# Relu² attention feeding a capacity-routed FFN: paired heads on TensorE tiles, whole-batch loads, an on-chip broadcast and a hand-written issue order

## The chip, the core and the metric

The kernel runs on one core of a Trainium2 chip. The metric is device time in microseconds of one execution; lower is better. Three runs of the kernel before gave 380.47, 383.15 and 383.99 us, with a median of 383.15 us.

## What is computed

Eight batches, 12 heads of 448 tokens with head dimension 64. The attention has no softmax: the scores are clipped at zero and squared. Its output, laid out as 448 tokens of 768 features, is the input x of a mixture-of-depths layer: a gate vector scores each token, the 128 best tokens of each batch go through a two-matrix FFN, and their result, scaled by the sigmoid of the score, is added to x.

```python
scores = np.matmul(q, k.transpose(0, 1, 3, 2)) / 8
attn = np.maximum(scores, 0.0) ** 2 / 448
x = np.matmul(attn, v)                      # heads side by side: 8 x 448 x 768
s = np.einsum('bsd,d->bs', x, w_gate)
top = 128 tokens of largest s, per batch
out = x.copy()
out[top] += sigmoid(s[top]) * (np.maximum(x[top] @ w1, 0) @ w2)    # w1 768x1024, w2 1024x768
```

## The kernel before

The unit of work is a pair of heads: six pairs per batch, 48 in all. Tokens are cut into four chunks of 112 (`NCH`, `P`), four tokens of a row to a partition.

`load_qkv_pair` issues three DMAs per pair from POOL's queue, which also convert float32 to bf16: q and k as 112 partitions of eight 64-element pieces (L104 for the first two pairs, in four DMAs each; L106 else), v as 112 partitions of two 256-element pieces (L107). The FFN weights `w1_sb` and `w2_sb` (L84, L86) are loaded behind the first pair's data.

`attention_pair` transposes q and k of both heads on TensorE (L121, eight products of 112 columns against the identity) and copies the result to SBUF on VectorE (L129). Then each head in turn makes its scores, two chunks of keys to a PSUM tile `s_psum` (L140: 64 contraction rows, 112 keys, 448 queries); ScalarE clips the tile (L150; every twelfth on VectorE, L153), VectorE squares it (L156), and TensorE multiplies it into `oT_psum` (L161: 112 rows, 64 output columns, 448 queries), the first head into partitions 0 to 63, the second into 64 to 127. ScalarE copies the pair's output to `xT_sb` (L167).

`assemble_x` makes the gate scores as one row (L173), copies the row out of PSUM (L179), stores it to DRAM (L180) and transposes x back to token order (L186, copied by VectorE in L192). `moe_batch` reads the scores back from DRAM twice, as columns (L196) and broadcast to 128 partitions (L199); VectorE counts each token's rank (L206) and makes a one-hot matrix (L214), which TensorE transposes (L220, copied in L227); L231 and L235 make the sigmoid. Then TensorE gathers the 128 tokens (L244, copied by ScalarE in L249) and runs the FFN (L259, relu L264; L272, scaled copy L277). The result is scattered back by a product with the transposed one-hot (L284), added to x on VectorE (L289), and x is stored by POOL's queue (L297; the last batch in four pieces, L295).

Nothing in the text sets the order between these parts: the tile framework's scheduler orders each engine's instructions by priority and free buffers (`qk` 4, `qt` 3, `s_psum` 2, `m_psum` 2), and every DMA of POOL's queue uses one of eight semaphores in turn, so that a DMA is issued only when the eighth before it has landed.

Of the kernel before, what the change touches and what calls it, by code (L numbers as in the profile page):

```python
# [9 lines left out]
FP32 = mybir.dt.float32  # L10
# [4 lines left out]
ALU = mybir.AluOpType  # L15


@with_exitstack
def kernel(
# [11 lines left out]
    nc = tc.nc  # L31
# [6 lines left out]
    NCH = S // P  # L38
    NDC = HD // 128
    NFC = F // 128  # L40
    assert S == NCH * P

    o_scale = 1.0 / (Dh * S)

    RELU_DVE_EVERY = 12
    SQUARE_2TILE = True

    const_pool = ctx.enter_context(tc.tile_pool(name="const", bufs=1))
    qk_pool = ctx.enter_context(tc.tile_pool(name="qk", bufs=4))
    qt_pool = ctx.enter_context(tc.tile_pool(name="qt", bufs=3))  # L50
    a_pool = ctx.enter_context(tc.tile_pool(name="a", bufs=5))
    xt_pool = ctx.enter_context(tc.tile_pool(name="xt", bufs=2))
    x_pool = ctx.enter_context(tc.tile_pool(name="x", bufs=2))
    moe_pool = ctx.enter_context(tc.tile_pool(name="moe", bufs=3))
    small_pool = ctx.enter_context(tc.tile_pool(name="small", bufs=3))

    qt_psum_pool = ctx.enter_context(tc.tile_pool(name="qt_psum", bufs=1, space=bass.MemoryType.PSUM))
    s_psum_pool = ctx.enter_context(tc.tile_pool(name="s_psum", bufs=2, space=bass.MemoryType.PSUM))
    o_psum_pool = ctx.enter_context(tc.tile_pool(name="o_psum", bufs=1, space=bass.MemoryType.PSUM))
    m_psum_pool = ctx.enter_context(tc.tile_pool(name="m_psum", bufs=2, space=bass.MemoryType.PSUM))  # L60

# [12 lines left out]

    iotac_i32 = const_pool.tile([128, 1], INT32)
    nc.gpsimd.iota(iotac_i32, pattern=[[0, 1]], base=1, channel_multiplier=1)
    slot_col = const_pool.tile([128, 1], FP32)
    nc.vector.tensor_copy(out=slot_col, in_=iotac_i32)

    w1_sb = const_pool.tile([128, NDC, F], BF16)  # L80
    w2_sb = const_pool.tile([128, NFC, HD], BF16)

    def load_moe_weights():
        nc.gpsimd.dma_start(out=w1_sb,  # L84
                            in_=moe_w1.rearrange("(m p) f -> p m f", p=128))
        nc.gpsimd.dma_start(out=w2_sb,  # L86
                            in_=moe_w2.rearrange("(m p) f -> p m f", p=128))

    scores_dram = dram_pool.tile([B, S], FP32)

    out_ch = out.rearrange("b (p four) d -> b p four d", four=NCH)

    def load_qkv_pair(b, hp):
        h0 = 2 * hp
        qp = qk_pool.tile([P, NCH, 2, Dh], BF16, name="qp")
        kp = qk_pool.tile([P, NCH, 2, Dh], BF16, name="kp")
        vp = qk_pool.tile([P, 2, NCH, Dh], BF16, name="vp")
        split_load = (b == 0 and hp < 2)
        for t_sb, t_dram in ((qp, q), (kp, k)):
            src_ap = t_dram[b, h0:h0 + 2].rearrange(  # L100
                "hh (p four) d -> p four hh d", four=NCH)
            if split_load:
                for c in range(NCH):
                    nc.gpsimd.dma_start(out=t_sb[:, c], in_=src_ap[:, c])  # L104
            else:
                nc.gpsimd.dma_start(out=t_sb, in_=src_ap)  # L106
# [239 lines left out]
```

## Time and profile before

| | |
|---|---|
| median of 3 runs | 383.15 us (380.47 to 383.99) |
| the profiled execution, first to last instruction (span) | 403.7 us |
| TensorE busy (its matmuls), weight loads | 354.8 us (88%), 169.2 us |
| VectorE, ScalarE, GpSimd busy | 237.0 us (59%), 209.1 us (52%), 157.1 us (39%) |
| DMA packets, data | 108188, 32.91 MB |

The profiled execution is one run under the hardware profiler, and its span is longer than the median by 20.5 us; the trace shows nothing outside the span. Busy time is the time in which an engine had an instruction under way. Matmuls overlap and their ends are modelled, so a busy TensorE is not one at its peak. GB/s counts the bytes written, which for a load that converts are half of those read.

### The profile page before, as it was taken

The numbers are of one execution on the slowest core, as the hardware profiler recorded it, in microseconds if no ns is written. First come the engines' busy times: TensorE is split into PE (matmuls) and PEld (weight loads), VectorE is DVE, ScalarE is ACT, GpSimd is POOL, SyncE is SP. The second block draws the span as 40 slices with busy tenths as digits, with TensorE's granted clock in tenths as the row PEclk, the third lists the DMA queues.
The fourth block names the chain that finished last, engine by engine and source line by source line (L and its number), as shares of the span: only waits on it lengthen the run. The fifth ranks groups of instructions, "written<-read, shape, count | busy, mean of one in ns | idle before, by whom it ended". The sixth has DMA issues, their size and how long they took to land.

```text
span 403.7 us, 5755 instructions
## 1 busy us (share of the span) xinstructions
PE 354.8 (88%) x2192; PEld 169.2 (42%) x2192; DVE 237.0 (59%) x474; ACT 209.1 (52%) x290; POOL 157.1 (39%) x178
## 2 busy tenths in 40 slices
PE   1717999999999999998999999999999999997483
PEld 0202333343644464445434543455345534542271
DVE  0302453345466876678468846874688468946423
ACT  1403354444565846683657565846576657655121
POOL 9419655412034813571158225720573063000002
PEclk9999999999999999998999999989999999999568
DMA  5999999536029952995199809970899199103004
GB/s 26 171 168 99 75 74 65 45 38 57 2 22 194 111 41 23 194 109 42 12 195 100 62 11 198 99 61 11 185 85 87 13 185 82 21 2 136 23 2 137
DMA packets 108188, 32.91 MB, mean 82 GB/s; under 512 B 93353, under 2 KB 106161, under 8 KB 107377
## 3 DMA queue, kind: packets, MB, share of 16 engines
q0 software_dynamic: 103280, 30.68, 66.1%
q1 hardware_dynamic: 4880, 1.86, 2.3%
q8 instruction: 17, 0.28, 0.3%
q14 instruction: 11, 0.08, 0.1%
HBM read 41.17 MB, written 11.02 MB: 129 GB/s over the span
## 4 chain that ended last, share of the span: by engine, by line
PE 51%; issue 17%; DMA 13%; DVE 10%; POOL 5%; ACT 2%; POOLq 0%; SPq 0%; DVEq 0%
PE s_psum L140 14%; PE oT_psum L161 13%; DMA scores_bc<-scores_dram 6%; DMA w_sb<-in_moe_w_dram 5%; PE hT_psum L259 4%; PE ye_psum L272 4%; PE qt_psum L121 4%; PE delta_psum L284 3%; DVE a_sb L156 3%; PE xeT_psum L244 3%; DVE cmp_trash L206 3%; PE x_psum L186 2%; PE sc_psum L173 2%; DVE qkt L129 2%; DVE t_sb L153 1%
## 5 line engine op out<-in xcount | busy, mean ns | idle before, releaser
L150 ACT ACTIVATE t_sb<-s_psum 112x896 bf16<-112x896 f32 x176 | 155.1, 916 | 84.7 <-PE s_psum L140 80.0
L156 DVE TENSOR_TENSOR a_sb<-t_sb 112x896 bf16<-112x896 bf16 x192 | 113.6, 620 | 49.5 <-ACT t_sb L150 49.4
L140 PE MATMUL s_psum<-qkt 64*112 64x448 bf16 x384 | 118.6, 416 | 4.6 <-ACT t_sb L150 2.5
L161 PE MATMUL oT_psum<-a_sb,vp 112*64 112x448 bf16 x384 | 104.1, 405 | 7.3 <-ACT xT_sb L167 4.4
L107 POOL DMA_DIRECT2D vp<-in_v_dram x48 | 42.6, 888 | 118.2 <-PE oT_psum L161 110.5
L106 POOL DMA_DIRECT2D qp<-in_q_dram x46 | 62.1, 1356 | 47.5 <-PE qt_psum L121 47.2
L106 POOL DMA_DIRECT2D kp<-in_k_dram x46 | 71.7, 1580 | 10.9 <-PE qt_psum L121 9.1
L289 DVE TENSOR_TENSOR x_sb<-delta_psum,x_sb 112x384 bf16<-112x384 f32 x64 | 34.6, 556 | 47.9 <-PE delta_psum L284 46.4
L140 PEld LDWEIGHTS <-qkt 64*112 64x112 bf16 x384 | 39.0, 137 | 56.5 <-issue 46.6
L129 DVE COPY qkt<-qt_psum 128x896 bf16<-128x896 bf16 x48 | 29.8, 620 | 36.9 <-PE qt_psum L121 33.8
L161 PEld LDWEIGHTS <-vp 112*64 112x64 bf16 x384 | 29.0, 115 | 47.2 <-issue 37.7
L167 ACT ACTIVATE xT_sb<-oT_psum 128x448 bf16<-128x448 f32 x48 | 26.1, 544 | 38.7 <-PE oT_psum L161 38.1
L121 PE MATMUL qt_psum<-ident,qp 112*128 112x112 bf16 x192 | 23.4, 231 | 16.3 <-DMA qp<-in_q_dram 16.2
L121 PEld LDWEIGHTS <-qp 112*128 112x128 bf16 x192 | 13.5, 104 | 37.0 <-DMA qp<-in_q_dram 18.3
L121 PE MATMUL qt_psum<-ident,kp 112*128 112x112 bf16 x192 | 25.1, 231 | 3.4 <-DMA kp<-in_k_dram 3.2
L249 ACT CAST xeT_sb<-xeT_psum 128x384 bf16<-128x384 f32 x16 | 7.6, 477 | 36.7 <-PE xeT_psum L244 36.7
L259 PE MATMUL hT_psum<-xeT_sb,w_sb 128*128 128x128 bf16 x384 | 25.9, 227 | 0.2 <-ACT xeT_sb L249 0.2
L192 DVE COPY x_sb<-x_psum 112x768 bf16<-112x768 bf16 x32 | 17.2, 554 | 13.9 <-PE x_psum L186 13.3
L259 PEld LDWEIGHTS <-w_sb 128*128 128x128 bf16 x384 | 23.6, 103 | 3.0 <-issue 3.0
L206 DVE TENSOR_SCALAR_CACHE_REDUCE cmp_trash<-scores_bc,scores_cols 112x448 bf16<-112x448 f32 x32 | 21.6, 674 | 4.8 <-DMA scores_bc<-scores_dram 4.8
L186 PE MATMUL x_psum<-ident,xT_sb 128*112 128x128 bf16 x192 | 23.5, 250 | 0.3 <-ACT scores_row L179 0.3
L272 PE MATMUL ye_psum<-w_sb,hT_sb 128*128 128x384 bf16 x128 | 23.5, 327 | 0.3
(40 smaller groups left out, 226.9 us busy)
## 6 DMA issues: line engine op xcount, KB each, us to landing
out_dram<-x_sb POOLq DMA_DIRECT2D x7, 1344.0 KB, 6.4
vp<-in_v_dram POOLq DMA_DIRECT2D x48, 112.0 KB, 3.9
qp<-in_q_dram POOLq DMA_DIRECT2D x46, 112.0 KB, 3.7
kp<-in_k_dram POOLq DMA_DIRECT2D x46, 112.0 KB, 4.3
w_sb<-in_moe_w_dram POOLq DMA_DIRECT2D x2, 1536.0 KB, 16.1
scores_bc<-scores_dram SPq DMA_DIRECT2D x8, 224.0 KB
out_dram<-x_sb POOLq DMA_DIRECT2D x4, 336.0 KB, 2.6
qp<-in_q_dram POOLq DMA_DIRECT2D x8, 28.0 KB, 9.9
```

The source lines that it names most:

```text
L106: nc.gpsimd.dma_start(out=t_sb, in_=src_ap)
L107: nc.gpsimd.dma_start(out=vp, in_=v[b, h0:h0 + 2].rearrange("hh (p four) d -> p hh four d", four=NCH))
L121: nc.tensor.matmul(out=qt_psum[:, tno, c * P:(c + 1) * P], lhsT=t_all[:, c, :, :], rhs=ident[:P, :P], is_transpose=True, start=(i_tr == 0) ...
L129: nc.vector.tensor_copy(out=qkt, in_=qt_psum)
L140: nc.tensor.matmul(out=s_psum[:, u, :S], lhsT=kt[rows, jc * P:(jc + 1) * P], rhs=qt[rows, :], start=True, stop=True)
L150: nc.scalar.activation(out=t2_sb, in_=s_psum[:, :, :S], func=AF.Relu)
L156: nc.vector.tensor_tensor(out=a2_sb, in0=t2_sb, in1=t2_sb, op=ALU.mult)
L161: nc.tensor.matmul(out=oT_psum[rows, :], lhsT=vp[:, hh, jc, :], rhs=a2_sb[:, u, :], start=(jc == 0), stop=(jc == NCH - 1))
L206: nc.vector.tensor_scalar(out=cmp_trash, in0=scores_bcast, scalar1=scores_cols[:, c:c + 1], scalar2=None, op0=ALU.is_ge, op1=ALU.add, accu ...
L259: nc.tensor.matmul(out=hT_psum[:, fc, :], lhsT=w1_sb[:, m, fi * 128:(fi + 1) * 128], rhs=xeT_sb[:, m, :], start=(m == 0), stop=(m == NDC - 1))
L272: nc.tensor.matmul(out=ye_psum, lhsT=hT_sb[:, fi, :], rhs=w2_sb[:, fi, dd0:dd0 + ddn], start=(fi == 0), stop=(fi == NFC - 1))
L289: nc.vector.tensor_tensor(out=x_sb[:, c, dd0:dd0 + ddn], in0=delta_psum, in1=x_sb[:, c, dd0:dd0 + ddn], op=ALU.add)
```

## The change

The kernel is written anew. In the parts that matter here:

- Chunks of keys are 128 rows. 448 keys are three and a half chunks; the half chunks of two heads share the fourth, one in partitions 0 to 63 and the other in 64 to 127, with zeros in the other half (`zero_halves`).
- Scores of two heads are issued next to each other, one on contraction rows 0 to 63 and one on 64 to 127 (L180); the shared chunk is one product over all 128 rows (L184). The products with v alternate between output partitions 0 to 63 and 64 to 127 (L204). The transposes do so too, with 64 columns of weights (L159, L165).
- q, k and v are loaded a batch at a time into three sets of buffers, in nine DMAs of 256- or 192-element pieces (`load`); the first batch in three parts. The weights stand behind batch 0 and before batch 1, and batch b+2 is loaded when batch b starts.
- The gate weights are repeated over 128 columns (`wg_rep`), so that the scores come out on all 128 partitions (L221, L224); the columns are made by four small transposes (L239). The scores' trip through DRAM goes away.
- x is stored before the FFN (L269). The FFN's result is added to the 128 rows in DRAM by a scatter-add DMA (L330), whose row numbers are a product of the one-hot with token numbers (L280 to L287). The products and additions of L284 and L289 go away, as do the one-hot's transposes.
- Every relu is on ScalarE (L192), every square on VectorE (L193).
- The order of issue is the order of the text (`manual_schedule`): per pair t the scores of chunks 0 and 1, the rest of the pair before, the transposes of pair t+1, a piece of the FFN of the batch before, the scores of chunks 2 and 3, the first half of its own v products, another piece. `moe(b)` is a generator that yields the cost of each piece, and `advance` runs pieces as credit allows.

```diff
+    NBUF = 3
+    def load_q(b, h0, h1):
+        nc.gpsimd.dma_start(out=q_sb[b % NBUF][:, h0:h1],
+            in_=q[b, h0:h1].rearrange("h (p c) d -> p h c d", c=NC))
+    def load_kv(t_sb, src, b, h0, h1):
...
+        for par in range(2):
+            hs = slice(h0 + par, h1, 2)
+            lo, hi = (4, 3) if par == 0 else (3, 4)
+            nc.gpsimd.dma_start(out=t[0:64, hs, 0:lo, :],
+                in_=src[b, hs, 0:64 * lo].rearrange("h (p c) d -> p h c d", c=lo))
+            nc.gpsimd.dma_start(out=t[64:128, hs, 0:hi, :],
+                in_=src[b, hs, 64 * lo:S].rearrange("h (p c) d -> p h c d", c=hi))
...
+    load(0, 2, 6)
+    load(0, 6, H)
...
+    nc.gpsimd.dma_start(out=w1_sb, in_=moe_w1.rearrange("(m p) f -> p m f", p=128))
+    nc.gpsimd.dma_start(out=w2_sb, in_=moe_w2.rearrange("(m p) f -> p m f", p=128))
+    load(1, 0, H)
...
+    def transposes(t):
...
+        for c in range(NC):
+            for hh in range(2):
+                nc.tensor.matmul(out=ps[64 * hh:64 * hh + 64, c * P:(c + 1) * P],
+                                 lhsT=qs[:, h0 + hh, c, :], rhs=ident[:P, :P], is_transpose=True,
...
+    def scores(t, c):
...
+        if c < 3:
+            for hh in range(2):
+                rows = slice(64 * hh, 64 * hh + 64)
+                nc.tensor.matmul(out=ps[:, hh, :S], lhsT=sb[rows, S + c * 128:S + (c + 1) * 128],
+                    rhs=sb[rows, :S], start=True, stop=True)
+        else:
+            nc.tensor.matmul(out=ps[:, 0, :S], lhsT=sb[:, S + 384:S + 512],
+                             rhs=sb[:, :S], start=True, stop=True)
+    def attend(t, c):
...
+        for hh in range(2):
+            rows = slice(64 * hh, 64 * hh + 64)
+            nc.tensor.matmul(out=o_ps[t][rows, :], lhsT=vs[:, 2 * hp + hh, c, :],
+                             rhs=a[:, hh if c < 3 else 0, :], start=(c == 0),
...
+    def moe(b):
+        for m in range(NM):
+            nc.tensor.matmul(out=sc_ps, lhsT=wg_rep[:, m, :], rhs=xTb[:, m, :],
+                             start=(m == 0), stop=(m == NM - 1))
+        nc.scalar.copy(out=bc, in_=sc_ps)
+        yield 1.1
...
+            nc.vector.scalar_tensor_tensor(
+                out=trash, in0=bc[:P, :], scalar=cols[:, c:c + 1], in1=tie[:, c, :],
+                op0=ALU.subtract, op1=ALU.is_ge, accum_out=rank[:, c:c + 1])
...
+        nc.gpsimd.dma_start(out=out[b].rearrange("(p c) d -> p c d", c=NC), in_=x_sb)
...
+        nc.gpsimd.indirect_dma_start(out=out.rearrange("b s d -> (b s) d"),
+            out_offset=bass.IndirectOffsetOnAxis(ap=idx[:, :1], axis=0),
+            in_=gye, in_offset=None, element_offset=b * S * HD, compute_op=ALU.add)
...
+    MOE_US = 9.7
+        share = MOE_US / (2 * NHP) * 1.05
+        for t in range(NT + 1):
+            b, hp = divmod(t, NHP)
+            if t < NT:
+                scores(t, 0)
+                scores(t, 1)
+                relu_square(t, 0)
+                relu_square(t, 1)
+            if t > 0:
+                attend(t - 1, 2)
+                attend(t - 1, 3)
+                if t % NHP == 0:
+                    active.append(moe(t // NHP - 1))
+            if t < NT:
+                if hp == 0 and b + 2 < B:
+                    load(b + 2, 0, H)
+                if t + 1 < NT:
+                    transposes(t + 1)
+                advance(share)
+                scores(t, 2)
+                scores(t, 3)
...
+                attend(t, 0)
+                attend(t, 1)
+                advance(share)
```

TensorE in the kernel before, the first pair: `s_psum_146` takes two chunks of the first head's scores (from the transposed q and k in `qkt`), `s_psum_155` two of the second head's, and then the first head's products with v begin.

```order
L140 LDWEIGHTS qkt_134
L140 MATMUL s_psum_146<-qkt_134 112x448
L140 LDWEIGHTS qkt_134
L140 MATMUL s_psum_146<-qkt_134 112x448
L140 LDWEIGHTS qkt_134
L140 MATMUL s_psum_155<-qkt_134 112x448 [waits Activation_49]
L140 LDWEIGHTS qkt_134
L140 MATMUL s_psum_155<-qkt_134 112x448
L161 LDWEIGHTS vp_115 [waits DMASW1_49]
L161 MATMUL oT_psum_136<-a2_sb_140,vp_115 64x448 [waits DVE_49]
```

TensorE now, the second pair of batch 1 (t = 7): the scores of chunk 2 for both heads, those of the shared chunk 3, and the v products of chunks 0 and 1.

```order
L180 LDWEIGHTS qkt_585
L180 MATMUL s_ps_705<-qkt_585 128x448 [waits Activation_49]
L180 LDWEIGHTS qkt_585
L180 MATMUL s_ps_705<-qkt_585 128x448
L184 LDWEIGHTS qkt_585
L184 MATMUL s_ps_708<-qkt_585 128x448 [waits Activation_49]
L204 LDWEIGHTS v_sb1_96
L204 MATMUL o_ps_718<-a_sb_643,v_sb1_96 64x448 [waits Activation_49]
L204 LDWEIGHTS v_sb1_96
L204 MATMUL o_ps_718<-a_sb_643,v_sb1_96 64x448
```

Neighbouring products now belong to different heads, and each group of them is of another tile shape than the group before it: half the rows, all rows, half the columns.

POOL's queue in the kernel before, at the start: the weights, the second pair (in pieces) and the third, each DMA behind a semaphore of an earlier one.

```order
L84 DMA w1_sb_108<-in_moe_w1_dram 128x6x1024 [waits DMASW2_49]
L86 DMA w2_sb_109<-in_moe_w2_dram 128x8x768 [waits DMASW3_49]
L104 DMA qp_176<-in_q_dram 112x2x64 [waits DMASW4_49]
...
L104 DMA kp_177<-in_k_dram 112x2x64 [waits DMASW3_49]
L107 DMA vp_178<-in_v_dram 112x2x256 [waits DMASW4_49]
L106 DMA qp_237<-in_q_dram 112x8x64 [waits DMASW5_49]
```

POOL's queue now: the weights, batch 1, (batch 2 follows), the loads of batch 3, and behind them the first small casts of batch 0's routing (`tok0`, from the score columns `cols`) and its store.

```order
L117 DMA w1_sb_146<-in_moe_w1_dram 128x6x1024 [waits DMASW4_49]
L118 DMA w2_sb_147<-in_moe_w2_dram 128x8x768 [waits DMASW5_49]
L80 DMA q_sb1_94<-in_q_dram 112x12x256 [waits DMASW6_49]
L89 DMA k_sb1_95<-in_k_dram 64x6x256 [waits DMASW7_49]
...
L80 DMA q_sb0_91<-in_q_dram 112x12x256 [waits DMASW0_49,PE_49]
L89 DMA k_sb0_92<-in_k_dram 64x6x256 [waits DMASW1_49,PE_49]
...
L92 DMA v_sb0_93<-in_v_dram 64x6x256 [waits DMASW0_49,PE_49]
L245 CAST tok0_174<-cols_628 112x4 [waits DVE_49]
...
L269 DMA out_0_dram<-x_sb_587 112x3072 [waits DMASW1_49,DVE_49]
```

Where a pair's three DMAs stood, a batch's nine stand, and the routing's casts stand behind the last of the nine, which waits for the first of them to land.

## Rows read from the trace of the kernel before

**Rows 1.** Busy time of each engine in one batch period of the middle (windows).
```profile
core 0: us, PE busy (x) PEld busy (x) DVE busy (x) ACT busy (x) POOL busy (x), PEclk, DMA share, GB/s
140.60:181.50 40.90, 39.28 (x280) 19.41 (x278) 29.38 (x60) 26.33 (x38) 19.23 (x21) 1.00 0.80 92
```

**Rows 2.** TensorE, single products by turns: start us, us, operation, count (timeline).
```profile
155.31 0.38 PE L161 MATMUL oT_psum<-a_sb,vp 112*64 112x448 bf16 x1
155.62 0.39 PE L140 MATMUL s_psum<-qkt 64*112 64x448 bf16 x1
155.94 0.37 PE L284 MATMUL delta_psum<-gye_sb,onehotT 128*112 128x384 bf16 x1
```

**Rows 3.** TensorE, four attention products in a row, late in the span (timeline).
```profile
341.84 0.73 PE L140 MATMUL s_psum<-qkt 64*112 64x448 bf16 x4
342.50 0.73 PE L161 MATMUL oT_psum<-a_sb,vp 112*64 112x448 bf16 x4
...
368.33 0.96 PE L140 MATMUL s_psum<-qkt 64*112 64x448 bf16 x4
```

**Rows 4.** TensorE, products of the gather and the FFN, batch 6 (timeline).
```profile
349.77 0.84 PE L244 MATMUL xeT_psum<-onehot,x_sb 112*128 112x128 bf16 x12
...
351.23 2.69 PE L259 MATMUL hT_psum<-xeT_sb,w_sb 128*128 128x128 bf16 x45
353.75 2.98 PE L272 MATMUL ye_psum<-w_sb,hT_sb 128*128 128x384 bf16 x16
```

**Rows 5.** Groups by line: busy us, mean ns of one | idle before, releaser.
```profile
L150 ACT ACTIVATE t_sb<-s_psum 112x896 bf16<-112x896 f32 x176 | 155.1, 916 | 84.7 <-PE s_psum L140 80.0
L156 DVE TENSOR_TENSOR a_sb<-t_sb 112x896 bf16<-112x896 bf16 x192 | 113.6, 620 | 49.5 <-ACT t_sb L150 49.4
...
L129 DVE COPY qkt<-qt_psum 128x896 bf16<-128x896 bf16 x48 | 29.8, 620 | 36.9 <-PE qt_psum L121 33.8
...
L167 ACT ACTIVATE xT_sb<-oT_psum 128x448 bf16<-128x448 f32 x48 | 26.1, 544 | 38.7 <-PE oT_psum L161 38.1
...
L192 DVE COPY x_sb<-x_psum 112x768 bf16<-112x768 bf16 x32 | 17.2, 554 | 13.9 <-PE x_psum L186 13.3
...
L206 DVE TENSOR_SCALAR_CACHE_REDUCE cmp_trash<-scores_bc,scores_cols 112x448 bf16<-112x448 f32 x32 | 21.6, 674 | 4.8 <-DMA scores_bc<-scores_dram 4.8
```

**Rows 6.** Groups of weight loads, of 64 and of 128 columns.
```profile
L161 PEld LDWEIGHTS <-vp 112*64 112x64 bf16 x384 | 29.0, 115 | 47.2 <-issue 37.7
...
L259 PEld LDWEIGHTS <-w_sb 128*128 128x128 bf16 x384 | 23.6, 103 | 3.0 <-issue 3.0
```

**Rows 7.** The first third: one window, then two rows of TensorE's timeline.
```profile
60.00:106.00 46.00, 46.00 (x165) 18.39 (x165) 22.36 (x45) 20.79 (x28) 14.75 (x15) 1.00 0.57 46
...
97.22 1.74 PE L140 MATMUL s_psum<-qkt 64*112 64x448 bf16 x4
...
107.17 2.69 PE L259 MATMUL hT_psum<-xeT_sb,w_sb 128*128 128x128 bf16 x45
```

**Rows 8.** The start: POOL's and TensorE's timeline, then two windows of DMA.
```profile
21.78 0.66 POOL L104 DMA_DIRECT2D kp<-in_k_dram  x1 [7.35 <-DMA w_sb<-in_moe_w_dram]
...
29.24 0.86 PE L121 MATMUL qt_psum<-ident,qp 112*128 112x112 bf16 x4 [9.41 <-DMA qp<-in_q_dram]
...
20.00:25.00 5.00, 0.00 (x0) 0.00 (x0) 0.00 (x0) 0.00 (x0) 0.66 (x1) 1.00 1.16 211
50.00:55.00 5.00, 5.00 (x25) 2.01 (x24) 2.03 (x5) 1.93 (x3) 2.80 (x3) 1.00 1.57 99
```

**Rows 9.** The end, in order of time (timeline; SPq is the queue of SyncE).
```profile
375.03 0.54 ACT L167 ACTIVATE xT_sb<-oT_psum 128x448 bf16<-128x448 f32 x1 [3.55 <-PE oT_psum L161]
...
376.74 0.23 SPq L180 DMA_DIRECT2D scores_dram<-scores_row  x1
...
381.59 0.68 DVE L206 TENSOR_SCALAR_CACHE_REDUCE cmp_trash<-scores_bc,scores_cols 112x448 bf16<-112x448 f32 x1 [1.98 <-DMA scores_bc<-scores_dram]
...
394.50 0.33 PE L284 MATMUL delta_psum<-gye_sb,onehotT 128*112 128x384 bf16 x1
...
399.46 0.52 POOL L295 DMA_DIRECT2D out_dram<-x_sb  x1 [0.45 <-DVE x_sb L289]
```

More of the change, by code (lines that the diff above doesn't have):

```diff
@@ L5 @@
 import concourse.tile as tile
-from concourse import bass_utils, mybir
+from concourse import mybir
 from concourse.masks import make_identity
@@ L37 @@
     P = 112
[L38 to L41, printed above, removed]
+    NC = S // P
+    NM = HD // 128
+    NF = F // 128
+    NHP = H // 2
+    NT = B * NHP
+    assert S == 448 and Dh == 64 and CAP == 128
     o_scale = 1.0 / (Dh * S)
[L45 to L49, printed above, removed]
+    const = ctx.enter_context(tc.tile_pool(name="const", bufs=1))
@@ L91 @@
-    out_ch = out.rearrange("b (p four) d -> b p four d", four=NCH)
-    def load_qkv_pair(b, hp):
-        h0 = 2 * hp
[L95 to L106, printed above, removed]
-        nc.gpsimd.dma_start(
-            out=vp,
-            in_=v[b, h0:h0 + 2].rearrange(
-                "hh (p four) d -> p hh four d", four=NCH))
-        return qp, kp, vp
@@ L299 @@
-    for b in range(B):
-        xT_sb = xt_pool.tile([128, NDC, S], BF16, name="xT_sb")
-        x_sb = x_pool.tile([P, NCH, HD], BF16, name="x_sb")
-        for hp in range(H // 2):
-            qp, kp, vp = load_qkv_pair(b, hp)
-            attention_pair(b, hp, qp, kp, vp, xT_sb)
-            if b == 0 and hp == 0:
-                load_moe_weights()
-        assemble_x(b, xT_sb, x_sb)
-        moe_batch(b, x_sb)
+    moe_pool = ctx.enter_context(tc.tile_pool(name="moe", bufs=2))
+    small = ctx.enter_context(tc.tile_pool(name="small", bufs=2))
@@ new lines @@
+    s_ps_pool = ctx.enter_context(tc.tile_pool(name="s_ps", bufs=2, space=PSUM))
+    t_ps_pool = ctx.enter_context(tc.tile_pool(name="t_ps", bufs=1, space=PSUM))
+    o_ps_pool = ctx.enter_context(tc.tile_pool(name="o_ps", bufs=1, space=PSUM))
+    m_ps_pool = ctx.enter_context(tc.tile_pool(name="m_ps", bufs=2, space=PSUM))
+    NBUF = 3
+    q_sb, k_sb, v_sb = [], [], []
+    for i in range(NBUF):
+        q_sb.append(const.tile([P, H, NC, Dh], BF16, name=f"q_sb{i}"))
+        k_sb.append(const.tile([128, H, 4, Dh], BF16, name=f"k_sb{i}"))
+        v_sb.append(const.tile([128, H, 4, Dh], BF16, name=f"v_sb{i}"))
@@ new lines, in load @@
+    def load(b, h0, h1):
+        load_q(b, h0, h1)
+        load_kv(k_sb, k, b, h0, h1)
+        load_kv(v_sb, v, b, h0, h1)
+    load_q(0, 0, 2)
+    load_kv(k_sb, k, 0, 0, 2)
+    ident = const.tile([128, 128], BF16)
+    make_identity(nc, ident)
+    zero_halves(0)
+    load_kv(v_sb, v, 0, 0, 2)
+    load(0, 2, 6)
+    load(0, 6, H)
+    for i in range(1, NBUF):
+        zero_halves(i)
+    wg_cols = const.tile([128, NM], BF16)
+    nc.gpsimd.dma_start(out=wg_cols, in_=moe_w_gate.rearrange("(m p) -> p m", p=128))
@@ new lines, with advance @@
+    MOE_US = 9.7
+    active = []
+    credit = [0.0]
+    def advance(us):
+        if not active:
+            credit[0] = 0.0
+            return
+        credit[0] += us
+        while active and credit[0] > 0.0:
+            try:
+                credit[0] -= next(active[0])
+            except StopIteration:
+                active.pop(0)
+    tc_manual = tc.manual_schedule()
+    with tc_manual:
+        transposes(0)
+        share = MOE_US / (2 * NHP) * 1.05
+        for t in range(NT + 1):
+            b, hp = divmod(t, NHP)
+            if t < NT:
[16 more added lines that the diff above has]
+                scores(t, 3)
+                relu_square(t, 2)
+                relu_square(t, 3)
+                attend(t, 0)
+                attend(t, 1)
+                advance(share)
+        while active:
+            advance(10.0)
```

364 lines of the change are left out of this document (172 added, 192 removed).

## The prediction

> **What bounds the kernel now.** I read the windows first, then TensorE's timeline inside one window, then the groups by line, then the start and the end. In a batch period of 40.9 us TensorE is busy 39.3, VectorE 29.4 and ScalarE 26.3 [rows 1]: TensorE bounds the middle. But its busy time is not streaming alone. Where single products follow each other with a change of tile shape (64 columns, then 64 rows, then the full array), they start 0.31 and 0.32 us apart [rows 2]; four of one shape on one tile take 0.96 us, the last of them modelled at 0.39, so they start 0.19 us apart [rows 3]. A change of shape costs 0.12 us. And in two rows four attention products take 0.73 us instead of 0.96 [rows 3]: there the second and the third belong to different heads, so to different halves of the array, and start together. That is what the change wants to have everywhere, and the trace shows it at work on rows (L140) and on columns (L161).
>
> The first third is another regime. From 60 to 106 us TensorE is busy all 46 us, and four score products take 1.74 us there against 0.96 late in the span [rows 3, 7]: they run at the lower of the two clocks, 1.2 GHz, though the clock column prints 1.00. The FFN's dense products of batch 0 start at 107.17 us and run 0.056 us apart [rows 7], which is full speed. Attention alone had not raised the clock in 46 us.
>
> The start is DMA. The second pair's q, issued behind the weights, holds TensorE for 9.4 us until 29.2 us, and POOL itself waits 7.35 us for a weight DMA whose semaphore it wants to use again [rows 8]. Queue order is landing order.
>
> **TensorE per pair after the change.** Scores: three products side by side plus the shared chunk, 4 x 0.19 = 0.76 us, where eight in a row were 1.5. Products with v: four side by side, 0.76. Transposes: 16 products of 112 or 128 columns on two halves, so eight times 0.053 = 0.43 us (0.056 is the spacing of 128-column products in [rows 4, 7]); if they don't overlap, 0.86. One sixth of the FFN's batch: h 48 x 0.056 = 2.7, y 16 x 0.17 = 2.8, gather 24 x 0.06 = 1.4, x transposes 24 x 0.056 = 1.4, scores 6 x 0.19 = 1.1, small ones 0.3, together 9.7 us [rows 4] or 1.62 per pair. The pair's order has seven changes of shape (rows, columns, full, rows, full, columns, full): 7 x 0.12 = 0.84. Sum 4.4 us per pair, 26.5 per batch. The transposed one-hot, the delta products and their adds (64 of 0.55 us on VectorE) are gone.
>
> The others fit below that. ScalarE, every relu now: three of 0.84 (three in a row at 0.916 each less their overlap), half of one at 0.45, the output copy 0.54 [rows 5], and a sixth of the FFN's seven copies of about 0.55 plus the sigmoid: 0.7. Sum 4.2 us. VectorE: transposed q and k 0.65, three squares of 0.62 and half of one, 2.2, and a sixth of four x copies (0.55), four rank counts (0.76 with the accumulator read), and 1.4 for one-hot and small copies, 1.1. Sum 3.95.
>
> **What the fixed order adds.** The instructions of one pair are not spread evenly. In the second pair of a batch VectorE has two squares, the qk copy, three rank counts with three x copies between them (3.9 us), two squares, the last rank count and the one-hot: 1.24 + 0.65 + 3.9 + 0.95 + 0.76 + 1.0 = 8.5 us. TensorE, in order, wants the one-hot 1.35 pairs after that pair began, at 5.9 us; behind its wait stand the gather and the next scores, for which ScalarE then waits. So 2.6 us are lost per batch, less only if TensorE is late anyway (bound 0), more if the sigmoid, which waits for four small POOL operations and stands in ScalarE's queue ahead of two relus, adds its own 1.5 us (bound 4). I take 2.7: 29.2 us per batch, 4.86 per pair, where the trace of before has 40.9 per batch.
>
> **The start.** POOL issues 27 DMAs for batch 0 at about 0.66 us each [rows 8], until 18.5 us. The weights are 3.1 MB written; at 211 GB/s [rows 8] they land by 34.5. A batch's q, k and v are 2.06 MB in 512- and 384-byte writes. The trace has two rates near: 211 GB/s for the weights' long rows, 99 GB/s for q and k in 128-byte pieces [rows 8], so 10 to 21 us a batch. I take 14, nearer to the long rows, since the packets grow fourfold. Then batch 1's k lands at 44, batch 1 at 48.5, batch 2 at 62.5. The first batch's pairs are through by about 35 and TensorE waits for batch 1's k till 45. Behind that comes a chain in POOL's queue: the nine DMAs of batch 3 stand ahead of batch 0's routing casts, and the ninth may issue only when the first of the nine (q, 4.7 us of data) has landed behind batch 2: 62.5 + 4.7 + 2 for the landing, 0.7 for the ninth issue and 1.5 for five casts: 71.5 us. TensorE waits for those casts at the selection product, 2.35 pairs into batch 1. By its own pace it would come there at 45 + 2.9 pairs of 8 us at half clock = 68, so the queue decides by little, and I set 72 us. Bounds: 60 with 10 us per batch and the clock up early, 88 with 21 us.
>
> **The end.** In the kernel before the last pair's copy starts at 375.0, and the end is at 403.7: 28.7 us. The trip of the scores through DRAM (376.74 to 381.59, 4.9 us) becomes four small transposes and a copy, about 0.8. Deltas, adds and four stores (394.5 to 399.46, 5.0 us) [rows 9] become one scatter-add; no row shows one. Its nearest rows are the store's issue of 0.52 us and the 4.2 us from the last issue to the end; it reads as well as writes and has 128 row numbers to look up: 0.5 to 10 us, I take 2 on top of the 4.2. The x copies now stand between the rank counts, +1.7, and the last squares and v products come late, +1.5. 28.7 - 4.1 - 5.0 + 2 + 1.7 + 1.5 = 25; with the small copies 26 us.
>
> **Sum.** 72 us to the first selection, then 48 - 8.35 = 39.65 pairs of 4.86 us = 193, and 26: 291 us of span, against 403.7 now. The medians of runs without the profiler stand at 383.15 / 403.7 = 0.949 of the profiled span. I scale: 276 us.
>
> The Trainium skill speaks against one term. The row first: loads of 64 weight columns take 115 ns each in the mean, loads of 128 columns 103 [rows 6], so half the columns is not half the time. The Trainium skill, "TensorEngine Tiling (Array Packing)", Restrictions, says that column tiling disables the fast weight load, which agrees with that row. The Trainium skill, "TensorE: Matmul & The Clock Gate", LDWEIGHTS (loading the stationary operand), puts a load at its columns divided by 1.2; by that figure 64 columns are an estimated 53 ns, and 16 of them per pair 0.85 us, where I have 0.43 for the transposes. By this rule the sum would be 0.42 x 39.65 = 17 us longer. The 115 ns overlap with products in [rows 6] and don't say how closely loads can follow.
>
> **The rivals.** (1) TensorE is never kept waiting by the order: 4.4 us per pair, 72 + 175 + 26 = 273, scaled 259. For it: the squares and relus of one half pair fall beside the other half's products. Against: VectorE's 8.5 us in one pair. (2) The transposes' weight loads come one after another: +17, 308, scaled 292. For it [rows 6]; against, products of 128 columns run 0.056 apart with a load each [rows 4]. (3) Pairs start together only now and then: scores and v products up to 1.33 us more, 6.2 per pair, 344, scaled 326. Against: [rows 3]. (4) Slower than before: TensorE stays at 1.2 GHz. The clock rose in the kernel before with 5 us of FFN products in one piece [rows 7, 4]; the change cuts these into pieces of 12 between attention groups. At half clock a pair is 2 x 3.57 + 7 x 0.12 = 8.0 us, and the end 6 us longer: 72 + 317 + 32 = 421, scaled 400. It decides from about 36 of the 39.65 pairs at that clock. Against: the second half of the gather and the first FFN piece stand together, 24 products in a row. A third of the pairs at half clock gives 291 + 41 = 332, scaled 315. (5) The change does not do what it says, in that the POOL queue's order makes every batch wait as the first does: load issue 8 us and q's landing put the casts 9.5 to 10.5 us into a batch, and the selection comes at 2.35 x 4.86 = 11.4. It would cost up to 2 us per batch with 21 us loads, +16 at the start: 321, scaled 305.
>
> **How the numbers follow.** Forecast 0.50 (its own 264 to 289), rival 1 0.15, rival 2 0.13, rival 3 0.05, a part at half clock 0.08, all at half clock 0.04, rival 5 0.05. From 248 (a start of 60 with rival 1: 261 scaled) to 312 all but part of rivals 3 and 4 are inside. About 1% is what a measurement of this kernel can tell from no change. Only rival 4 ends on the far side: faster 0.95, same 0.01, slower 0.04.
>
> **What would show it.** Right: TensorE's score rows two to a start, a batch period near 29 us in the windows, TensorE waiting for a DMA of k around 35 to 45 us and for POOL's casts around 70, and some 26 us from the last output copy to the end. Wrong: four products of a pair at 0.96 us, 448-column products of 0.47 us past 100 us, TensorE waiting for POOL in every batch, or a tail above 34 us.

## The result and the profile after

| | before | after |
|---|---|---|
| median | 382.84 us (380.47 to 383.99, 4 runs) | 314.76 us (312.75 to 315.93, 4 runs) |
| ratio | | 0.8236, 95% interval 0.8172 to 0.8299 |
| span of the profiled execution | 403.7 us | 314.2 us (its own time 315.93) |

Faster, as forecast, but 38.8 us slower than the 276 forecast, and 2.8 us above the upper end of the range. Of 21 runs of the kernel before that were taken beside the experiments, three took 401 to 406 us (none of them traced), one 394.88, and the others 379 to 386. The middle first: two windows of the changed kernel that make up one batch period, from one selection product to the next (columns as in [rows 1]).

```profile
171.50:190.60 19.10, 19.10 (x217) 10.81 (x217) 9.32 (x18) 15.42 (x26) 1.78 (x6) 0.92 0.30 87
190.60:205.00 14.40, 9.14 (x100) 5.09 (x99) 12.16 (x27) 8.75 (x14) 9.66 (x15) 1.00 1.16 149
```

The period is 33.5 us, against 40.9 in [rows 1] and 29.2 in the forecast. From selection to selection the seven periods are 35.9, 34.3, 34.2, 33.5, 31.4, 32.8 and 25.6 us; the first four end in a wait for POOL, and in the last no attention is left. In the first window, gather and FFN with their attention, TensorE is never idle. In the second, from the next batch's gate scores to its selection, it is idle for 5.3 us. TensorE's timeline in this period shows both parts:

```profile
171.56 1.44 PE L300 MATMUL xe_ps<-hot,x_sb 112*128 112x128 bf16 x12
...
180.29 0.55 PE L180 MATMUL s_ps<-qkt 64*128 64x448 bf16 x4
180.77 0.57 PE L204 MATMUL o_ps<-a_sb,v_sb 128*64 128x448 bf16 x4
181.17 0.37 PE L159 MATMUL t_ps<-ident,q_sb 112*64 112x112 bf16 x8
181.37 0.39 PE L165 MATMUL t_ps<-ident,k_sb 128*64 128x128 bf16 x8
181.70 0.84 PE L311 MATMUL h_ps<-xeT,w_sb 128*128 128x128 bf16 x12
...
197.26 0.49 PE L230 MATMUL x_ps<-ident,xT_sb 128*112 128x128 bf16 x6 [0.99 <-DVE cols L242]
...
204.97 0.24 PE L280 MATMUL sel_ps<-tok,hot 112*128 112x5 bf16 x4 [3.80 <-POOL tok L250]
```

Four attention products take 0.55 and 0.57 us where one shape on one tile took 0.96 [rows 3]. Sixteen transposes stand 0.53 us apart from what follows (181.17 to 181.70). The last row is what costs: TensorE idles 3.8 us at the selection product, and the profile names POOL's cast as the releaser. VectorE's one-hot, its other operand, was ready before that:

```profile
202.02 0.69 DVE L273 TENSOR_TENSOR hot<-slot_row,rank 112x512 bf16<-112x512 f32 x1
```

So some 1.6 of the 3.8 us belong to the one-hot (it ends at 202.7) and the rest to POOL. About half of that rest is the first cast's own length, 1.32 us here; it takes 1.3 to 1.6 us in three of the five batches with such a wait and 0.21 in the other two, and the cause stays open. What POOL did meanwhile shows best where it happens earlier, at the selection of batch 1:

```profile
92.96 1.41 POOL L89 DMA_DIRECT2D v_sb<-in_v_dram  x1
100.91 0.66 POOL L92 DMA_DIRECT2D v_sb<-in_v_dram  x1 [6.53 <-DMA q_sb<-in_q_dram]
101.56 0.21 POOL L245 CAST tok<-cols 112x4 bf16<-112x4 f32 x1
...
102.66 0.20 POOL L250 CAST tok<-rem 112x4 bf16<-112x4 f32 x1
```

The ninth DMA of batch 4's load waits 6.5 us for the first of the nine, q, to land; the routing casts stand behind it in POOL's queue. This is the chain that the prediction's sum has at the start only (its rival 5 has it in every batch). In the table of waits it is the second and the third row. The first, ScalarE's wait for the sigmoid's operand, comes one step later in the same chain:

```profile
ACT g L291 <- POOL g L290: 38.6, 8, 7.0
POOL v_sb L92 <- DMA q_sb<-in_q_dram: 21.3, 5, 6.5
...
PE sel_ps L280 <- POOL tok L250: 18.5, 5, 4.1
```

The start and the end, from the timeline: TensorE's wait for batch 1's k, ScalarE's last output copy and the last scatter-add.

```profile
46.39 0.60 PE L165 MATMUL t_ps<-ident,k_sb 128*64 128x128 bf16 x7 [1.58 <-DMA k_sb<-in_k_dram]
...
287.56 0.54 ACT L210 ACTIVATE xT_sb<-o_ps 128x448 bf16<-128x448 f32 x1
...
306.13 1.63 POOL L330 DMA_INDIRECT out_dram<-gye,idx  x1 [9.83 <-ACT gye L327]
```

Batch 1's k holds TensorE until 46.4 us (forecast 45), the first selection product starts at 67.0 (forecast 72), and from the last output copy to the end are 26.6 us (forecast 26).

### The profile page after: what moved, and what is told of

Same layout as the page of the kernel before. It is cut to its first block, busy times and chain, and to the rows that moved or that the text cites. A ratio compares the mean times of both kernels' runs of the same rounds, so it can differ in the third digit from the quotient of the medians.

```text
span 314.2 us, 6208 instructions
## 1 busy us (share of the span) xinstructions
PE 238.0 (76%) x2496; PEld 134.4 (43%) x2496; DVE 176.6 (56%) x378; ACT 196.6 (63%) x306; POOL 103.8 (33%) x191
## 4 chain that ended last, share of the span: by engine, by line
PE 28%; issue 24%; DMA 24%; POOL 11%; DVE 6%; ACT 4%; POOLq 1%; ACTq 0%; DVEq 0%
DMA q_sb<-in_q_dram 13%; DMA k_sb<-in_k_dram 7%; PE o_ps L204 7%; PE s_ps L180 5%; PE h_ps L311 4%; PE ye_ps L323 4%; DMA out_dram<-x_sb 3%; ACT r_sb L192 3%; DVE trash L257 2%; PE xe_ps L300 2%; POOL v_sb L92 2%; PE s_ps L184 2%; DVE x_sb L233 2%; POOL tok L245 2%; POOL k_sb L89 1%
## 5 line engine op out<-in xcount | busy, mean ns | idle before, releaser
L192 ACT ACTIVATE r_sb<-s_ps 128x896 bf16<-128x896 f32 x192 | 148.2, 829 | 50.7 <-PE s_ps L180 49.5
L193 DVE TENSOR_TENSOR a_sb<-r_sb 128x896 bf16<-128x896 bf16 x192 | 103.6, 563 | 86.6 <-ACT r_sb L192 86.2
L204 PE MATMUL o_ps<-a_sb,v_sb 128*64 128x448 bf16 x384 | 61.6, 397 | 2.0 <-DVE a_sb L193 1.7
L330 POOL DMA_INDIRECT out_dram<-gye,idx x8 | 13.4, 1674 | 130.7 <-ACT gye L327 130.7
L180 PE MATMUL s_ps<-qkt 64*128 64x448 bf16 x288 | 50.0, 383 | 2.2 <-ACT r_sb L192 1.0
L170 DVE COPY qkt<-t_ps 128x960 bf16<-128x960 bf16 x48 | 31.2, 650 | 20.2 <-PE t_ps L165 20.2
L159 PE MATMUL t_ps<-ident,q_sb 112*64 112x112 bf16 x384 | 19.4, 224 | 20.0 <-DMA q_sb<-in_q_dram 14.5
L204 PEld LDWEIGHTS <-v_sb 128*64 128x64 bf16 x384 | 18.6, 112 | 32.1 <-issue 26.3
L311 PE MATMUL h_ps<-xeT,w_sb 128*128 128x128 bf16 x384 | 28.1, 227 | 1.3 <-ACT xeT L302 1.3
L159 PEld LDWEIGHTS <-q_sb 112*64 112x64 bf16 x384 | 17.6, 118 | 26.3 <-DMA q_sb<-in_q_dram 20.1
L92 POOL DMA_DIRECT2D v_sb<-in_v_dram x20 | 16.5, 824 | 36.8 <-DMA q_sb<-in_q_dram 21.3
L210 ACT ACTIVATE xT_sb<-o_ps 128x448 bf16<-128x448 f32 x48 | 26.6, 554 | 0.0
L291 ACT ACTIVATE g<-g 128x1 f32<-128x1 f32 x8 | 1.6, 203 | 38.6 <-POOL g L290 38.6
L323 PE MATMUL ye_ps<-w_sb,hT 128*128 128x384 bf16 x128 | 24.9, 328 | 0.0
L180 PEld LDWEIGHTS <-qkt 64*128 64x128 bf16 x288 | 12.8, 95 | 28.4 <-issue 20.4
L165 PE MATMUL t_ps<-ident,k_sb 128*64 128x128 bf16 x384 | 21.4, 229 | 3.8 <-DMA k_sb<-in_k_dram 3.8
L257 DVE SCALAR_TENSOR_TENSOR trash<-bc,cols,tie 112x448 bf16<-112x448 f32 x32 | 21.6, 675 | 0.2
L89 POOL DMA_DIRECT2D v_sb<-in_v_dram x20 | 19.1, 958 | 7.0 <-DMA w_sb<-in_moe_w_dram 6.8
L280 PE MATMUL sel_ps<-tok,hot 112*128 112x5 bf16 x32 | 2.0, 168 | 25.5 <-POOL tok L250 18.5
## 6 DMA issues: line engine op xcount, KB each, us to landing
q_sb<-in_q_dram POOLq DMA_DIRECT2D x7, 672.0 KB, 10.1
k_sb<-in_k_dram POOLq DMA_DIRECT2D x14, 192.0 KB, 10.3
```

The lines of the kernel that those rows point to most:

```text
L92: nc.gpsimd.dma_start(out=t[64:128, hs, 0:hi, :], in_=src[b, hs, 64 * lo:S].rearrange("h (p c) d -> p h c d", c=hi))
L159: nc.tensor.matmul(out=ps[64 * hh:64 * hh + 64, c * P:(c + 1) * P], lhsT=qs[:, h0 + hh, c, :], rhs=ident[:P, :P], is_transpose=True, start ...
L170: nc.vector.tensor_copy(out=sb, in_=ps)
L180: nc.tensor.matmul(out=ps[:, hh, :S], lhsT=sb[rows, S + c * 128:S + (c + 1) * 128], rhs=sb[rows, :S], start=True, stop=True)
L192: nc.scalar.activation(out=r[:, :n], in_=ps[:, :n, :S], func=AF.Relu)
L193: nc.vector.tensor_tensor(out=a[:, :n], in0=r[:, :n], in1=r[:, :n], op=ALU.mult)
```

## The experiments

Theory Q: the routing casts stand behind a load's ninth DMA, in every batch that still loads. Its rivals: H, VectorE's rank counts make the one-hot late; P, TensorE's own work paces the batch; S and B on the start; G on the sigmoid; C and N on whether products of two heads run side by side. The letters mean what each expectation says.

**The load behind the casts.**

```diff
-                if hp == 0 and b + 2 < B:
+                if hp == 3 and b + 2 < B:
                     load(b + 2, 0, H)
```

> The nine load DMAs of batch b+2 are issued at the fourth pair of batch b, behind the routing's POOL operations, where the changed kernel issues them at the first pair, ahead of them. Theory Q (the routing casts stand behind the ninth load, which waits for the first one to land): TensorE's wait for POOL's tok at the selection product, 18.5 us in five batches, goes; in those batches tok came 3.4, 3.1, 2.0, 2.0 and 2.0 us after the one-hot, so 12.5 us are won: 302 us. Rival H (VectorE's rank counts and x copies make the one-hot late, POOL only hides behind it): under 4 us won, the wait for tok is replaced by an equally long one for hot. Rival P (TensorE's own work paces the batch): the waits go and come back elsewhere, 312 to 316 us.

Measured: 305.17 us (304.05 to 306.68), 9.6 us won of the 12.5 expected; ratio to before 0.8001 (0.7906 to 0.8096). One batch period (window), then TensorE's timeline in it:

```profile
183.10:214.70 31.60, 27.21 (x317) 15.50 (x314) 21.42 (x45) 24.09 (x40) 10.81 (x21) 1.00 0.73 123
```

```profile
195.31 0.26 PE L280 MATMUL sel_ps<-tok,hot 112*128 112x5 bf16 x4 [1.60 <-DVE hot L273]
195.43 0.83 PE L300 MATMUL xe_ps<-hot,x_sb 112*128 112x128 bf16 x12
...
199.38 0.80 PE L180 MATMUL s_ps<-qkt 64*128 64x448 bf16 x4 [1.25 <-ACT r_sb L192]
```

The wait for tok is gone and 1.6 us for the one-hot are left: Q holds, and H is next in line and not in Q's place. With the clock at 1.00 in the whole period TensorE's work is 27.2 us, and the twelve gather products take 0.83 us, where they took 1.44 after the 3.8 us wait. A new wait shows: the scores now wait 1.25 us for ScalarE's relu.

**Only q behind the casts**, the eight DMAs of k and v left in front.

```diff
                 if hp == 0 and b + 2 < B:
-                    load(b + 2, 0, H)
+                    load_kv(k_sb, k, b + 2, 0, H)
+                    load_kv(v_sb, v, b + 2, 0, H)
+                if hp == 3 and b + 2 < B:
+                    load_q(b + 2, 0, H)
```

> The changed kernel with the eight DMAs of k and v left at the first pair of the batch, ahead of the casts, and only the one of q issued at the fourth pair, so that no ninth DMA stands ahead of the casts. Theory Q9 (what holds the casts is the ninth issue, which waits until the first of the nine has landed): the casts come when the columns are there, as with all nine moved, 304 to 307 us. Rival Q8 (the eight issues of 0.66 us each and their place in the queue are enough to hold the casts): 311 to 315 us.

Measured: 304.41 us (303.12 to 306.77), the same as with all nine moved. POOL's timeline of one batch:

```profile
191.09 0.77 POOL L92 DMA_DIRECT2D v_sb<-in_v_dram  x1
191.93 0.20 POOL L245 CAST tok<-cols 112x4 bf16<-112x4 f32 x1
```

The last of the eight issues without a wait and the casts follow at once. It is the ninth DMA's wait for a landing that cost, not the place or the issue time of the other eight.

**The sigmoid late**, alone.

```diff
-        nc.scalar.activation(out=g, in_=g, func=AF.Sigmoid)
         yield 0.2
...
         gye = moe_pool.tile([CAP, HD], FP32, name="gye")
+        nc.scalar.activation(out=g, in_=g, func=AF.Sigmoid)
```

> The sigmoid is issued on ScalarE just before the scaled output copies instead of right after the selection. Theory Q: ScalarE's wait for POOL's g, 38.6 us in eight batches, is the same wait as TensorE's for tok seen one step later; moved, it costs nothing and brings nothing: 313 to 316 us. Rival G (the step of the prediction that gave the sigmoid up to 1.5 us per batch): the relus behind it come 1.5 us earlier in each of eight batches and TensorE follows, 12 us won: 303 us.

Measured: 314.34 us (311.94 to 316.07), no difference: the largest wait of ScalarE after the relus, 38.6 us, was worth nothing. That fits theory Q's time, but the wait is not only POOL's queue seen one step later: with the late load 28.3 of the 38.6 us are left. What holds the gain back, and when it comes, is below.

**The weights last**, alone.

```diff
+    load(1, 0, H)
     w1_sb = const.tile([128, NM, F], BF16)
...
-    load(1, 0, H)
```

> The loads of both FFN weights are issued behind batch 1's load instead of ahead of it. Theory Q: TensorE's wait for batch 1's k until 46 us goes, but the casts of batch 0 still stand behind batch 3's q, and the bytes queued ahead of that q are the same, so the first selection product stays at 65 to 67 us: 312 to 315 us. Rival S (the start is bound by the wait for batch 1's k): the first selection moves from 67.0 to about 58 us, and the whole kernel ends 8 to 9 us earlier: 306 us.

Measured: 312.98 us (312.30 to 313.69), 1.8 us less, about what a measurement can tell. TensorE's timeline shows where the gain went:

```profile
30.71 0.70 PE L165 MATMUL t_ps<-ident,k_sb 128*64 128x128 bf16 x8
...
47.40 0.39 PE L165 MATMUL t_ps<-ident,k_sb 128*64 128x128 bf16 x8
66.70 0.25 PE L280 MATMUL sel_ps<-tok,hot 112*128 112x5 bf16 x4 [18.91 <-POOL tok L250]
```

Batch 1's first transposes (30.71) no longer wait for its k, which came at 46.4 behind the weights, and TensorE then waits 18.9 us for POOL. The start has two waits, one behind the other.

**Both.** Late load and weights last, with batch 2's load behind batch 0's casts too.

```diff
-                if hp == 0 and b + 2 < B:
+                if hp == 3 and b > 0 and b + 2 < B:
+                    if b == 1:
+                        load(2, 0, H)
                     load(b + 2, 0, H)
```

> The late load and the FFN weights behind batch 1's load together; batch 2's load is issued at the fourth pair of batch 1 with batch 3's, so that nothing that waits stands ahead of batch 0's casts. Theory Q (each of the two start waits hid behind the other): the last scores of batch 0 end at 34.5 us, the one-hot follows 13 us later, the first selection product starts at 48 us where it started at 63.3 with the late load alone, and the kernel ends 15 us earlier: 290 us. Rival B (the start is bound by the bytes: w1 or batch 2 now lands too late): the first product with w1, or the first transposes of batch 2, wait, and half or more is given back: 297 to 305 us.

Measured: 289.15 us (286.67 to 291.62), 16.0 us less than with the late load alone, where the weights by themselves had given 1.8. The weights and batch 2's load moved together here, so the 16.0 us are not split between them. The four runs spread over 5 us, so this gain and the two that are measured from 289.15 are good to some 2 us. The first selection product, without a wait:

```profile
47.94 0.27 PE L280 MATMUL sel_ps<-tok,hot 112*128 112x5 bf16 x4
```

**The x copies on ScalarE**, with the late load.

```diff
-            nc.vector.tensor_copy(out=x_sb[:, c, :], in_=x_ps)
+            nc.scalar.copy(out=x_sb[:, c, :], in_=x_ps)
```

> The late load, and the four copies of the transposed x go from VectorE to ScalarE, so that VectorE's one-hot comes some 2 us earlier. Theory Q then H (with the queue out of the way TensorE waits for the one-hot, 11.4 us in seven batches with the late load): most of that is won, 295 us against 305.2 with the late load alone. Rival P (ScalarE, 24 us busy of 31.6 per batch, gets 2.8 more and the relus come late by as much): 303 to 307 us.

Measured: 298.33 us (296.68 to 299.52), 6.8 us won of 10. H is true of what was left, but only in part: TensorE's waits for the one-hot fall from 11.4 us in all to 8.9. The middle batch is no shorter (window):

```profile
177.60:209.20 31.60, 28.53 (x316) 16.05 (x312) 19.80 (x41) 26.62 (x43) 10.97 (x21) 0.95 0.73 123
```

Its period is 31.6 us as with the late load alone: the wait for the one-hot falls from 1.60 to 1.26 us, a transpose of x waits 1.33 us for ScalarE's copy where it waited 0.99 for the columns, and part of the batch is at half clock. The gain lies in the first selection (1.4 us earlier), the first three periods (33.7, 33.5 and 33.1 us become 32.7, 31.4 and 32.2) and the last two (1.7 us together); which wait brings it there is not shown.

**The sigmoid again, and the copies, on the kernel with load and start mended.**

> The late load, the weights behind batch 1 and the late sigmoid, with the x copies left on VectorE; beside 289.2 us without the late sigmoid and 273.5 us with the x copies on ScalarE as well. Theory S (with POOL's queue cleared, ScalarE's wait for g keeps the relus and through them TensorE 1.25 us in every batch, where in the changed kernel it lay inside the longer wait for tok): 8 to 9 us won, 280 us. Rival A (the sigmoid brings as little as it did alone, 0.4 us, and only both edits together free the stretch): 287 to 289 us.

Measured: 278.83 us (278.17 to 279.29), 10.3 us less than 289.15. The same edit was worth 0.4 us in the changed kernel.

> The late load, the weights behind batch 1 and the x copies on ScalarE, with the sigmoid left in its early place; beside 289.2 us without the copies moved. Theory S (the gains add, 6.8 us as between the two kernels with the late load, and the sigmoid's own 8 us are missing): 282 us. Rival A (only both edits together free the stretch, because the selection's chain and ScalarE's wait for g follow one another): 286 to 289 us.

Measured: 282.19 us (280.48 to 284.15), 7.0 us less than 289.15. As theory S of these two runs has it, the gains nearly add. TensorE after the selection, first without and then with the late sigmoid:

```profile
177.16 0.26 PE L280 MATMUL sel_ps<-tok,hot 112*128 112x5 bf16 x4 [1.60 <-DVE hot L273]
...
179.69 1.46 PE L300 MATMUL xe_ps<-hot,x_sb 112*128 112x128 bf16 x12
...
182.93 0.28 PE L311 MATMUL h_ps<-xeT,w_sb 128*128 128x128 bf16 x2
```

```profile
170.92 0.25 PE L280 MATMUL sel_ps<-tok,hot 112*128 112x5 bf16 x4 [1.60 <-DVE hot L273]
...
172.88 0.84 PE L299 MATMUL xe_ps<-hot,x_sb 112*128 112x128 bf16 x12
...
175.07 1.51 PE L310 MATMUL h_ps<-xeT,w_sb 128*128 128x128 bf16 x24
```

The stretch from selection to the first FFN product is 5.8 us with the early sigmoid and 4.2 with the late one. In the first, part of it ran at half clock (1.46 for twelve products, not 0.84), in the second none. Windows of four such stretches tell the two apart: the kernel with load and start mended in the batch before and in the one just shown, the same with the late sigmoid, and the changed kernel with the late sigmoid.

```profile
145.60:151.36 5.76, 4.44 (x60) 2.79 (x60) 2.68 (x7) 3.14 (x7) 3.53 (x8) 1.00 0.77 248
177.16:182.93 5.77, 5.70 (x59) 3.37 (x60) 2.69 (x7) 3.15 (x7) 3.54 (x8) 0.70 0.73 247
170.92:175.07 4.15, 4.15 (x60) 2.61 (x60) 2.58 (x6) 3.04 (x6) 2.27 (x6) 1.00 0.84 332
169.78:175.38 5.60, 5.60 (x59) 3.21 (x59) 1.09 (x3) 3.13 (x6) 1.32 (x5) 0.70 1.08 304
```

With the early sigmoid the stretch is 5.8 us at either clock: at full clock TensorE has 4.4 us of work and waits 1.25 for a relu behind the sigmoid, at a mean of 0.70 its products fill the same time. So the 1.6 us are the relus' lateness. By the last row this is also why the same edit was worth nothing in the changed kernel: there TensorE is partly at half clock behind the wait for POOL, and the stretch takes 5.6 us with the late sigmoid and 5.5 with the early one. These are single batches, and no run changed the clock alone.

**All four edits.**

> The late load, weights behind batch 1, the late sigmoid and the x copies on ScalarE together. If the gains add: 290 with the first two, 10 us for the one-hot (theory H) and 2 to 4 us for the sigmoid, behind which ScalarE's relus kept TensorE for 0.5 to 1.3 us per batch with the late load: 276 to 279 us. Rival P (TensorE's own 27 to 28 us per batch is the floor of eight batches): not below 283 us.

Measured: 273.46 us (273.25 to 273.59); ratio to before 0.7164 (0.7116 to 0.7213), and 41.3 us less than the changed kernel. One batch period:

```profile
187.50:217.50 30.00, 26.93 (x316) 15.27 (x312) 19.80 (x41) 26.82 (x44) 5.12 (x12) 1.00 0.22 60
```

TensorE and ScalarE are both busy 27 of 30 us. With the late sigmoid but without the moved copies the period was 30.0 us too (170.92 to 200.88). Rival P's floor of 283 us fell; the four gains add nearly in full (9.6, 16.0, 7.0 and 10.3 make 42.9).

**Heads one after the other.** Transposes of one head then of the other, and in each group of four both products of one head first; shown for the transposes, the score and v products likewise.

```diff
-        for c in range(NC):
-            for hh in range(2):
+        for hh in range(2):
+            for c in range(NC):
```

> The changed kernel with the two heads of a pair issued one after the other within each group (both products of one head, then both of the other; the eight or nine transposes of one head, then those of the other), so that only products in the middle of a group stand next to one of the other head. Theory C (neighbours on different tiles start together, which the order of the rows buys): a group of four products takes 0.74 instead of 0.55 us, the transposes of a pair 0.9 instead of 0.5 us, about 1.0 us per pair on TensorE, of which the 4.3 pairs of each batch in which TensorE never waits count: some 34 to 45 us more, 349 to 360 us. Rival N (the order of issue does not matter for TensorE, or its time lies under other engines): under 5 us more, 314 to 320 us.

Measured: 321.04 us (318.84 to 323.92), 6.3 us more, where theory C had 34 to 45. TensorE's timeline:

```profile
185.75 0.68 PE L194 MATMUL s_ps<-qkt 64*128 64x448 bf16 x4
186.37 0.61 PE L216 MATMUL o_ps<-a_sb,v_sb 128*64 128x448 bf16 x4
186.77 0.40 PE L159 MATMUL t_ps<-ident,q_sb 112*64 112x112 bf16 x8
186.97 0.43 PE L165 MATMUL t_ps<-ident,k_sb 128*64 128x128 bf16 x8
```

Eight transposes, four of one head and then four of the other, take 0.40 us as against 0.37 when they alternate; groups of four 0.61 and 0.68 as against 0.57 and 0.55. The score groups vary: at full clock 0.56 to 0.93 in this batch, 0.55 to 0.75 in the changed kernel's. The overlap is there without alternation, for the scores not in every group. Neither side's reading was right; the next run was made to tell them apart.

**Both heads on the same rows.**

```diff
             for hh in range(2):
-                rows = slice(64 * hh, 64 * hh + 64)
+                rows = slice(0, 64)
```

> The changed kernel with the 64-row score products of both heads on the same half of the array: the second head's scores are computed from the first head's q and k, so this part of the output is left out. Theory C (products on different tiles run at the same time, whatever their order): four score products take 0.93 us instead of 0.55, two take 0.55 instead of 0.36, 0.57 us more per pair, which counts in the 4.3 pairs of a batch where TensorE never waits: 17 to 27 us more, 332 to 342 us. Rival N (the side-by-side products save nothing, the time lies under ScalarE): 314 to 320 us.

Measured: 338.97 us (337.19 to 341.94), 24.2 us more. TensorE's timeline:

```profile
194.94 0.93 PE L180 MATMUL s_ps<-qkt 64*128 64x448 bf16 x4
...
197.50 0.55 PE L180 MATMUL s_ps<-qkt 64*128 64x448 bf16 x2
```

0.93 and 0.55 us, as expected. Side by side is real and worth some 24 us for the scores alone (a part of that is clock: its mean is 0.858 here and 0.898 in the changed kernel). It is the tile that buys most of it; the order of issue is the smaller part (6.3 us).

**The kernel before, once more.**

> The kernel before once more, unchanged, for its span beside its time. Theory: a span stands some 2 us under the time of its own run, as in the changed kernel (314.2 against 315.9 us), and 403.7 us belonged to one slow profiled execution: span 379 to 383 us. Rival (the prediction's scaling step): profiled executions of this kernel are 5% longer than the others: span 400 to 405 us beside a time of 383 us.

Measured: time 383.71 us, span 381.6. The window that answers to the first of [rows 7]:

```profile
60.00:106.00 46.00, 44.59 (x292) 21.33 (x293) 31.69 (x64) 30.19 (x43) 19.65 (x21) 1.00 0.74 86
...
63.13 0.96 PE L140 MATMUL s_psum<-qkt 64*112 64x448 bf16 x4
```

292 products in these 46 us, where [rows 7] has 165, and four score products in 0.96 us (timeline) where they took 1.74. The clock column prints 1.00 in both windows and the mean clocks are alike (0.964 here, 0.967 there); the half clock is read off the products' lengths. The profiled execution of 403.7 us, from which the prediction was made, ran at half clock until 107 us; this one until about 54 us (two score products take 0.99 us at 48.31 and 0.58 at 55.95), although its first FFN product comes only at 82.48. Its time of 383.71 us is the usual one.

## Why the prediction was wrong

Two steps failed, by 15 and by 28 us, and a third gave 5 back.

- **"I scale: 276 us"** (15 us). The 0.949 was taken for a difference between profiled and other runs. It was one execution's half clock in the first third; a span stands about 2 us under its own time (314.2 and 315.93, 381.6 and 383.71). Nothing of the kind was in the changed kernel's sum (half clock stood only in the 68 us that the queue's 72 beat), so there was nothing to scale. Unscaled, the sum was 291.
- **"4.86 per pair"** (28 us). From the first selection product (67.0) to the last output copy (287.6) are 220.6 us, the sum had 193. The step that failed is "What the fixed order adds", 2.7 us per batch for a late one-hot alone. Per batch of 33.5 us, against 29.2: TensorE's work at full clock was right, 27.2 against 26.5. Its groups at half clock after the wait, which the sum puts at nothing, add 1.0 (19.10 + 9.14 = 28.2), and its idle time is 5.3 where the sum had 2.7. Of that, 1.6 is the one-hot, 1.0 the score columns, of which the sum has nothing, and some 2.2 POOL's casts. The last part is the mechanism of rival 5, which had 0.05 and "up to 2 us per batch": the ninth issue was worked out for the first batch, and for later ones set against a selection 11.4 us into the batch, without asking when the one-hot is ready and how long q takes to land. It is issued right behind the scatter-add (191.22 and 190.13 us) and takes 10.1 us in the median of seven loads, where the start had 4.7 of data and 2 for the landing. The runs price the queue at 9.6 us in all. Of the 10.9 us between the two traces' spans 3.7 are the first selection (67.0 to 63.3) and 7.0 lie behind it (220.6 to 213.6), a quarter of the 28. With the queue clear a middle batch still takes 31.6 us, with 4.4 idle: the one-hot, the score columns and the 1.25 us for the relu.
- **The sigmoid's "own 1.5 us"**, which stood in the upper bound of 4 and hardly in the 2.7: 0.4 us in all in the changed kernel (inside the measurement), 10.3 us or 1.3 per batch with load and start mended. The size was right and a condition missing: by the windows above, that TensorE is not at half clock in that stretch.
- **The start, "I set 72 us"**: 67.0. The chain was the right one, ending in casts behind batch 3's loads, and k at 45 against 46.4; the loads were sized 5 us too slow. That both waits of the start hide each other was said ("the queue decides by little") and shown: 1.8 us for the weights alone, 16.0 for them and batch 2's load on top of the late load.
- **The end, "26 us"**: 26.6, partly by luck. From the scatter-add's issue to the end are 8.1 us, where the sum had 6.2, and the stretch before it is 18.6 where the sum leaves 19.8.
- **"Side by side"**: right in kind and size (0.55 and 0.57 us for four; sixteen transposes 0.53, forecast 0.43). Rival 2's longer transposes didn't come: an estimate from the load figure of the Trainium skill, "TensorE: Matmul & The Clock Gate", LDWEIGHTS (loading the stationary operand), had them at 0.85 us with the loads one after another, and the trace has 0.53.
- **Rival 4's half clock**: "attention alone had not raised the clock in 46 us" was true of that one execution. In the other traced execution of the kernel before it is full in that stretch, and it rose before the first FFN product: the long FFN piece, with which rival 4 has it rise, was not needed.

With the queue clear the period is 31.6 us, and with the late sigmoid as well 30.0, of which TensorE is busy 26.9 (forecast 26.5): the 29.2 forecast is close to what this kernel does without these two waits.

## What to carry to other kernels

An engine's queue is followed instruction by instruction through every stage, not only the one where it first hurts: a small operation behind a DMA that must wait for an earlier one to land is as late as that landing. The length of a wait is not what its removal brings; two waits that end together must both go, and a wait worth nothing today (38.6 us of ScalarE) can be the next bound. And when the profiled execution differs from the median, find the stretch that differs before scaling anything by it.

## What was not expected of the hardware

- TensorE overlaps products on different tiles although four of one tile are issued before the first of the other (0.40 us for eight transposes, 0.37 alternating). The Trainium skill, "TensorEngine Tiling (Array Packing)", Key Properties, says that tiles work independently; the trace agrees.
- After four of the changed kernel's five waits for POOL (3.0 to 4.1 us) TensorE comes back at 1.2 GHz: the first twelve gather products take 1.43 to 1.44 us, not 0.83 to 0.84, and the granted clock is 0.50 from 171.45 to 173.00. In the fifth they take 1.12. After 1.6 us for the one-hot it differs from batch to batch: with the late load 1.44 us at 130.56 and 0.83 at 195.31, and with load and start mended the clock falls only about 1 us after TensorE is back (1.00 from 177.10 to 178.20, 0.57 from 178.20 to 179.60). So a wait's cost can include the slower products behind it.
